# Window attention feeding a soft mixture of experts: value products over 128 keys at once, and expert weights fetched in pieces

## The chip, the cores and the metric

The kernel runs on one core of a Trainium2 chip. The metric is the device time of one execution in microseconds, the median of several runs. TensorE (PE) multiplies matrices, VectorE (DVE) and ScalarE (ACT) read its results out of PSUM, GpSimd (POOL) works on SBUF alone, and SyncE (SP) issues all the DMAs of this kernel.

## The reference

Attention over 4 batches, 8 heads, 768 positions of 64 numbers, in which a position sees the first 4 positions (sinks) and the 128 positions up to itself; its output, with the heads side by side, is the input of a soft mixture of 8 experts with 4 slots each. All is float32.

```
scores = scale * q @ k.T                       # per head, 768 x 768
keep   = (col < 4) | ((0 <= row - col) & (row - col < 128))
a      = exp(where(keep, scores, -1e9) - rowmax); a /= a.sum + 1e-9
x      = (a @ v) as 3072 x 512                  # (batch, position) x (head, dim)
logits = x @ phi                                # 3072 x 32
slot_input = softmax(logits over positions).T @ x   # 32 x 512
h      = relu(slot_input[e] @ w1[e]); slot_out = h @ w2[e]   # w1 512x1024, w2 1024x512
out    = softmax(logits over slots) @ slot_out
```

## The kernel before

**Stages.** From the start to about 211 us the kernel does the attention and the logits. The last 52 us, called the tail here, are the experts and the final product. The attention goes in 12 jobs `(b, j)`, three for each batch, of 256 positions and all 8 heads.

**One job** has these steps on PE. `prep` transposes k and q (rows `ident,first` from the buffer first_74). Four `scores` steps (S, rows `wt,qt`), each for 64 positions of both key blocks and 4 heads, go through `maxima` on DVE and `exps` on ACT. `weights_transposed` (T, rows `ident,wt`) turns the exponentials so that keys lie on partitions, and `select` on POOL makes two masked copies of them: `w = 1` for a block of 128 keys that holds the position itself, `w = 0` for the block before. `values` multiplies them by v (rows `banks<-wt 64x64`). `turned` transposes the result (rows `ident,first` from first_75), and `Moe.tokens` makes the logits (`first,phi` and `pst,vphi`), transposes them (`ident,lt`), and adds to the slots' inputs (`first,lb` and `sk,lb`). Steps of three jobs are interleaved.

**Halves of a block.** The window is 128 wide and a block of keys is 128, so for the 64 positions of half `o` one of the two blocks has all its 128 keys in play (`w = o`), and the other (`w = 1 - o`) has 64 of them; the masked remainder is zero.

**values, before.** All products have 64 keys (a quarter of the array, 64 x 64). A whole block takes two, in rows 0 to 63 and in rows 64 to 127. Two row halves must not write one PSUM bank side by side, so phase 0 pairs row half r with bank o = r and phase 1 with bank o = 1 - r. Where a phase 1 follows phase 0 of its own quad, it has a wait on some earlier DVE or ACT instruction (`guard`) or a drain of PE.

**What sets the order.** `Plan` holds a list of steps with a key (a due time, from the table `CFG`), a duration, and what each reads and writes. `Plan.order` lays them out on the engines by key and by readiness, and the program is issued in that order, with each engine's instructions in program order. All DMAs stand in the SP queue in order: a load that has to wait for a buffer holds up those behind it.

**Weights.** The 32 loads of 1 MB (w1 and w2, `Weights.load`) go to 24 buffers of 1 MB; 17 are steps of the plan, the others follow when attention's buffers come free, and the last 9 when the tail frees a buffer.

Of the kernel before, what the change touches and what calls it, by code (L numbers as in the profile page):

```python
# [19 lines left out]
P = 128  # L20
# [128 lines left out]
class Engine:  # L149


    def __init__(self, tc, engine):
        self.tc, self.engine, self.last = tc, engine, None

    def __getattr__(self, name):
        f = getattr(self.engine, name)

        def issue(*args, **kw):
            self.last = self.tc.keep_in_program_order(f(*args, **kw))  # L159
            return self.last  # L160

        return issue

# [10 lines left out]
class Plan:  # L174
# [11 lines left out]

    def __init__(self, banks):

        self.banks, self.steps, self.modes, self.aparts, self.handles, self.handed = banks, [], [], [], 0, 0

    def psum(self):
        self.handles += 1
# [15 lines left out]
    def add(self, key, eng, time, fn, r=(), w=(), new=None, last=None, mode=(128, 128), apart=None):  # L208
# [4 lines left out]
        self.aparts.append(apart)  # L213
        return len(self.steps) - 1

    def order(self):
        steps = self.steps
        writer, readers = {}, {}
        before, opener, later = [], {}, {}
        for i, (_, eng, _, _, r, w, new, last) in enumerate(steps):  # L220
            d = set()
            for x in r:
                d.add(writer.get(x, i))
                if x in opener:

                    d.update(readers.get(x, ())[-1:])
                readers.setdefault(x, []).append(i)
            for x in w:
                d.update(readers.get(x, ()))
                d.add(writer.get(x, i))  # L230
                writer[x], readers[x] = i, []
            d.discard(i)
            before.append(d)
            for x in new:
                opener[x["name"]] = i

            for x in r + w:
                if x in opener and eng != "P":
                    o = opener[x]
                    later.setdefault(o, set()).update(y for y in d if steps[y][1] == "P" and y != o and self.aparts[y] != o)  # L240
        self.before = before
# [6 lines left out]
        banks = [(0.0, i) for i in range(self.banks.shape[1])]  # L248
# [5 lines left out]
        while len(order) < len(steps):  # L254
# [27 lines left out]
            _, e, t0, i = best  # L282
            if e == "P":
                t0 += self.SWITCH * (self.modes[i] != mode)
                mode = self.modes[i][0:2]
            _, engs, times, _, _, _, new, last = steps[i]
            done.add(i)
            for x in engs:
# [13 lines left out]
            order.append((t0, len(order), i, e))  # L302
        return order

    def issue(self, engines):
        order = sorted(self.order())
        at, seen = {}, []
        end = max(t for t, _, i, e in order if e == "P" and self.steps[i][0] < self.IDLE)
        for t, _, i, e in order:
            _, _, _, fn, _, _, new, _ = self.steps[i]  # L310
            if t > end and self.steps[i][0] >= self.IDLE:
                continue
            for x in new:
                x["tile"] = self.banks[:, x["bank"]]
            if e == "P" and self.aparts[i] is not None:
                after = at[self.aparts[i]]
                self.guard = min(((z, ins) for z, p, ins in seen if p > after and z <= t), key=lambda x: x[0], default=(0, None))[1]
            fn(e)
            if e == "P":
                at[i] = len(at)  # L320
            elif e in "AV":
                p = max((at[y] for y in self.before[i] if self.steps[y][1] == "P"), default=-1)
                seen.append((t + self.steps[i][2][self.steps[i][1].index(e)], p, engines[e].last))


class InOrder(Plan):


    def add(self, key, eng, time, fn, r=(), w=(), new=None, last=None, mode=None, apart=None):
# [388 lines left out]
class Weights:  # L718
# [6 lines left out]
        self.order = first[:8] + second[:9] + first[8:] + second[9:]  # L725

    def load(self, t):
        kind, e, h = self.order[len(self.tiles)]
        if kind == 0:
            t2, w = t.rearrange("p (k m) -> p k m", k=2), self.w1[e:e + 2].rearrange("e (k p) m -> p e k m", p=P)[:, :, h, :]  # L730
        else:
            t2 = t.rearrange("p (k m) -> p k m", k=8)
            w = self.w2[e].rearrange("(p k) m -> p k m", p=P)[:, :, 256 * h:256 * h + 256]
        self.nc.sync.dma_start(t2, w)
        self.tiles.append(t)
        self.at[kind, e, h] = t


NSLOT = 24
WARM = 8, 10, 64  # L740
PT = 3
CFG = {'prep': [-2.99, 12.6],
 'load': [-5.66, -19.55],
 'v': [-1.2, -2.66],
 'S': -3.87,
 'M': -3.77,
 'E': -2.73,
 'N': [13.44, 53.07],
 'K0': -3.8,
 'T': [0.47, -19.7],  # L750
 'K': 29.21,
 'sel': [-17.71, 7.32, 4.91, 11.98],
 'val': [0.6, -4.15, 12.57, -13.52, -65.89],
 'xn': [1.21],
 'tok': [3.19, -16.24, 15.51, -3.34, 8.11, -1.71, -0.63, -5.02, 1.48, 1.1, 8.3],
 'sm': 1.41,
 'sinks': -2.62,
 'tr': [-31.47, 5.9, 6.73, -3.57, -49.94, -13.07, -0.19, 8.19, 6.09, -3.17, -12.06, 0.68, -1.67, -12.04,
        -4.42, 1.98, 59.56, -19.18, -20.81, 12.46, -40.38, -6.51, -6.05, 3.08, -20.05, 3.97, 63.44],
 'w': [33.2, 0.6],  # L760
 'fin': [8.45, 12.86, -4.85, -31.93, -19.39, -64.74, 1.63, -6.42, 62.33, 9.53, -17.38],
 'xn1': [21.29],
 'tok1': [17.06, -7.8, -20.78, 8.19, -2.53, 2.36, 1.06, -1.06, 3.59, 20.68, 1.52]}


def window_path(ctx, tc, c, moe, q, k, v, phi, w1, w2, out):
# [229 lines left out]
    def values(keys, n):  # L996
# [1 line left out]
        b, j = jobs[n]  # L998
        hs = plan.psum(), plan.psum()
        names = [h["name"] for h in hs]  # L1000
        prior = None

        def go(quad, phase):
            guard = plan.guard if phase > quad else None
            if phase > quad and guard is None:
                nc.tensor.drain()
            for a in range(4):
                y = 64 * (4 * quad + a)
                for w in (1, 0):
                    for r in range(2):  # L1010
                        o = r ^ phase
                        rows = slice(64 * r, 64 * r + 64)
                        for i in range(2):
                            if phase and w != o or (w == 0 and i == 0 and j == 0):
                                continue
                            ins = nc.tensor.matmul(
                                hs[o]["tile"][64 * i:64 * i + 64, y:y + 64],
                                lhsT=xws[quad][rows, i, w, a, 64 * o:64 * o + 64],
                                rhs=vbs[rows, (2 * n + i - 1 + w) % 4, 4 * quad + a, :],
                                start=(phase == 0 and quad == 0 and a == 0 and w == 1),  # L1020
                                stop=(phase == 1 and quad == 1 and a == 3), skip_group_check=True)
                            if guard:
                                tc.add_manual_dep(ins.ins, guard.ins.name, mybir.DependencyInfo(
                                    mybir.DependencyClass.Sync, mybir.DependencyReason.DATA), reason="row tiles")
                                guard = None

        for phase in range(2):
            for quad in range(2):
                r = [("xw", quad, i, w) for i in range(2) for w in range(2)]
                r += [("vb", x % 4) for x in range(2 * n - (j > 0), 2 * n + 2)]  # L1030
                turn = phase > quad
                prior = add(keys[2 * phase + quad], "P", 0.53 if phase else 1.0,
                            lambda e, quad=quad, phase=phase: go(quad, phase), r=r, w=names,
                            new=hs if not phase and not quad else None, mode=(*QUARTERS, 1) if turn else QUARTERS,
                            apart=prior if turn else None)
# [19 lines left out]
    def weight():  # L1055
        weights.load(slot())
# [48 lines left out]
            last = ["sit"] if b == B - 1 else []  # L1105
            moe.slot_softmax(plan, t(O["sm"]), b, [("lg", b, x, i) for x in range(NJ) for i in range(2)] + last)
    for i in range(NSLOT - 7):
        add(O["w"][0] + O["w"][1] * i, "D", 3.0, lambda e: weight())
# [14 lines left out]


def window_rest(tc, moe, plan, weight, weights, wts, slot, out):
    plan.issue({"A": moe.nc.scalar, "V": moe.nc.vector})

    def more(n):
        for _ in range(n):
# [213 lines left out]
```

## Time and profile before

| | before |
|---|---|
| median of 3 runs | 262.34 us (261.74 to 263.29) |
| the profiled execution: its time, its span | 265.25 us, 263.5 us |
| busy: PE, DVE, ACT, POOL | 216.1, 150.7, 135.4, 88.0 us |
| granted clock of TensorE, mean (1 is full speed) | 0.933 |
| DMA | 59.70 MB, 227 GB/s over the span |

The profiled execution is 2.91 us above the median, and 1.75 us of its time lie outside the span. A float32 matmul stands in the trace as two records of PE (MATMUL) and two of PEld (LDWEIGHTS); a transpose is one of each. A busy time is a sum over stages that have different limits, so the sections below go by stretches.

### The profile page before, as it was taken

How to read it: one execution, taken by the hardware profiler on the slowest of the kernel's cores; microseconds unless marked ns; L12 is line 12 of the kernel's file. 1: busy time of each engine (PE TensorE's matmuls, PEld its weight loads, DVE VectorE, ACT ScalarE, POOL GpSimd, SP SyncE). 2: the span in 40 equal slices, each digit the busy share in tenths (PEclk: the TensorE clock that was granted, in tenths of full speed). 3: DMA queues.
4: the chain of work that ended last, by engine and by line, in shares of the span. 5: the costliest groups of instructions: out<-in, count | busy, mean ns of one | idle time of the engine just before them, and what ended most of it. 6: DMA issues, size and time to landing. Idle time of an engine off the chain costs nothing.

```text
span 263.5 us, 12375 instructions
## 1 busy us (share of the span) xinstructions
PE 216.1 (82%) x5305; PEld 171.5 (65%) x5305; DVE 150.7 (57%) x368; ACT 135.4 (51%) x561; POOL 88.0 (33%) x223
## 2 busy tenths in 40 slices
PE   7679979998989778868699559958789999999820
PEld 7669857887868567757578458746669832586510
DVE  4387846888978558974459528864614331225230
ACT  2483956776767457772538437785423401224220
POOL 3133732725362443451308025351645205000000
PEclk9997999999999799995979968999979999999985
DMA  5598793889779892985729937999458769999995
GB/s 128 129 231 159 227 253 102 179 249 214 223 230 263 189 345 61 207 231 117 208 47 276 243 87 157 279 348 262 147 219 298 240 226 381 348 348 354 358 313 187
DMA packets 102979, 59.70 MB, mean 227 GB/s; under 512 B 76292, under 2 KB 98820, under 8 KB 102916
## 3 DMA queue, kind: packets, MB, share of 16 engines
q1 hardware_dynamic: 102916, 58.83, 79.4%
q8 instruction: 44, 0.72, 1.2%
q14 instruction: 19, 0.16, 0.2%
HBM read 52.53 MB, written 6.29 MB: 223 GB/s over the span
## 4 chain that ended last, share of the span: by engine, by line
PE 72%; issue 12%; DMA 5%; DVE 4%; ACT 2%; POOL 0%; DVEq 0%; ACTq 0%; POOLq 0%
PE banks L159 71%; DMA wt<-in_moe_w_dram 5%; ACT wt L159 2%; PE banks L1295 1%; DVE wt L695 1%; DVE wt L159 1%; DVE banks L159 1%; DVE first L159 1%; DVE acc L159 0%; ACT first L159 0%; DVE wt L680 0%; DVE qt L159 0%; ACT wt L679 0%; DVE si L159 0%; POOL ident masks.py:199 0%
## 5 line engine op out<-in xcount | busy, mean ns | idle before, releaser
L159 ACT ACTIVATE wt<-banks,wt 128x132 f32<-128x132 f32 x192 | 68.5, 374 | 32.3 <-DVE wt L159 22.5
L159 PE MATMUL banks<-wt 64*64 64x64 f32 (+2 forms) x2404 | 67.5, 248 | 11.6 <-issue 9.8
L159 PEld LDWEIGHTS banks<-wt 64*64 64x64 f32 (+2 forms) x2404 | 56.6, 140 | 24.1 <-issue 16.3
L159 PE MATMUL banks<-wt,qt 64*64 64x196 f32 (+2 forms) x780 | 50.4, 337 | 10.8 <-issue 7.1
L159 POOL TENSOR_SCALAR_AFFINE_SELECT wt<-wt 128x512 f32<-128x512 f32 x88 | 53.5, 634 | 14.2 <-ACT wt L159 11.6
L159 PEld LDWEIGHTS banks<-wt,qt 64*64 64x64 f32 x780 | 31.3, 140 | 15.6 <-issue 8.5
L159 ACT ACTIVATION_READ_ACCUMULATOR wt<-banks,wt 128x1 f32 x192 | 40.1, 209 | 0.0
L159 DVE TENSOR_REDUCE wt<-banks 128x4 f32<-128x528 f32 x48 | 34.0, 708 | 1.7
L159 POOL COPY sk<-wt 128x16 f32<-128x16 f32 x48 | 9.4, 197 | 72.8 <-ACT wt L159 69.5
L159 DVE COPY_PREDICATED banks<-later,banks 128x256 f32<-128x256 uint8 x48 | 20.4, 426 | 18.5 <-PE banks L159 15.2
L159 ACT COPY wt<-banks 128x512 f32<-128x512 f32 (+1 forms) x43 | 23.2, 576 | 14.5 <-PE banks L159 14.2
L159 PE MATMUL banks<-ident,first 64*128 64x64 f32 x576 | 25.5, 237 | 5.8 <-issue 4.7
L159 PEld LDWEIGHTS banks<-ident,first 64*128 64x128 f32 x576 | 22.2, 147 | 8.6 <-issue 5.3
L159 PE MATMUL banks<-ident,wt 64*128 64x64 f32 (+1 forms) x419 | 25.7, 246 | 1.2 <-issue 0.9
L159 PEld LDWEIGHTS banks<-ident,wt 64*128 64x128 f32 (+1 forms) x419 | 19.7, 150 | 8.9 <-issue 6.6
L159 DVE COPY wt<-banks 128x512 f32<-128x512 f32 (+2 forms) x34 | 21.8, 644 | 4.9 <-PE banks L159 2.6
L159 DVE TENSOR_TENSOR first<-banks,wt 128x512 f32<-128x512 f32 x24 | 15.4, 684 | 7.2 <-PE banks L159 6.8
L159 PE MATMUL banks<-first,phi 128*32 128x128 f32 x384 | 15.5, 307 | 3.9 <-issue 1.9
L159 PEld LDWEIGHTS banks<-first,phi 128*32 128x32 f32 x384 | 11.4, 122 | 5.3 <-ACT first L159 2.2
L159 PE MATMUL banks<-wt,si 128*32 128x512 f32 x112 | 14.1, 594 | 0.5 <-DVE si L159 0.5
L159 PE MATMUL banks<-neg,ident 64*64 64x68 f32 (+1 forms) x128 | 12.2, 248 | 0.2 <-issue 0.2
L159 DVE COPY first<-banks 128x512 f32<-128x512 f32 x12 | 8.2, 687 | 4.0 <-PE banks L159 3.9
(125 smaller groups left out, 228.2 us busy)
## 6 DMA issues: line engine op xcount, KB each, us to landing
wt<-in_moe_w_dram SPq DMA_DIRECT2D x30, 1024.0 KB, 9.2
wt<-in_v_dram SPq DMA_DIRECT2D x24, 256.0 KB, 4.5
first<-in_k_dram SPq DMA_DIRECT2D x22, 256.0 KB, 5.6
first<-in_q_dram SPq DMA_DIRECT2D x22, 256.0 KB, 4.6
out_dram<-wt SPq DMA_DIRECT2D x4, 1024.0 KB, 8.1
first<-in_moe_w_dram SPq DMA_DIRECT2D x2, 1024.0 KB
out_dram<-wt SPq DMA_DIRECT2D x3, 512.0 KB
first<-in_k_dram SPq DMA_DIRECT2D x4, 128.0 KB, 2.3
```

What stands on the lines that cost most here:

```text
L159: self.last = self.tc.keep_in_program_order(f(*args, **kw))
L695: (nc.vector.tensor_copy if n % 2 else nc.scalar.copy)(ob[:, 2 * (n - n0):2 * (n - n0) + 2], yp)
L1295: nc.tensor.matmul(t[:, 0:P], lhsT=c.ident, rhs=c.ident, start=True, stop=True)
```

## The change

1. `values` has four steps instead of two phases of two: for each quad `whole` multiplies the whole block with all 128 keys in one product (128 x 64 of the array) and `masked` multiplies the other with 64 keys (a quarter). The row half is o in both, so the banks need no pairing, and `guard` and the drain are gone, with the code that served them. The order is whole 0, masked 0, whole 1, masked 1.
2. A load of weights is 2 DMAs of 512 KB (w1) or 4 DMAs of 256 KB (w2), and each is a step of the plan of its own.
3. All the keys in `CFG` are other numbers, so all engines have another order. The first weights are due at 1.04 and then every 1.46, where they were due from 33.2 on, every 0.6.

```diff
-        def go(quad, phase):
-            guard = plan.guard if phase > quad else None
-            if phase > quad and guard is None:
-                nc.tensor.drain()
...
-                            if phase and w != o or (w == 0 and i == 0 and j == 0):
-                                continue
-                            ins = nc.tensor.matmul(
-                                hs[o]["tile"][64 * i:64 * i + 64, y:y + 64],
-                                lhsT=xws[quad][rows, i, w, a, 64 * o:64 * o + 64],
...
+        def product(quad, a, i, o, w, rows, start):
+            y = 64 * (4 * quad + a)
+            nc.tensor.matmul(hs[o]["tile"][64 * i:64 * i + 64, y:y + 64], lhsT=xws[quad][rows, i, w, a, 64 * o:64 * o + 64],
+                             rhs=vbs[rows, (2 * n + i - 1 + w) % 4, 4 * quad + a, :], start=start, stop=True,
+                             skip_group_check=True)
...
+                        if o or i or j:
+                            product(quad, a, i, o, o, slice(0, P), quad == 0 and a == 0)
...
+                        if not o or i or j:
+                            product(quad, a, i, o, 1 - o, slice(64 * o, 64 * o + 64),
+                                    quad == 0 and a == 0 and not (o or i or j))
...
+            add(keys[2 * quad], "P", 0.97, lambda e, quad=quad: whole(quad), r=r, w=names, new=None if quad else hs, mode=HALVES)
+            add(keys[2 * quad + 1], "P", 0.53, lambda e, quad=quad: masked(quad), r=r, w=names, mode=QUARTERS)
...
+            t, w = t[:, 1024 * x:1024 * x + 1024], self.w1[e + x, P * h:P * h + P]
...
+            t = t[:, 512 * x:512 * x + 512].rearrange("p (k m) -> p k m", k=2)
...
- 'val': [0.6, -4.15, 12.57, -13.52, -65.89],
+ 'val': [-7.87, 6.1, 1.92, -2.69, -35.19],
...
- 'w': [33.2, 0.6],
+ 'w': [1.04, 5.84],
```

How the steps of a job now stand on PE, in the middle of the program. Before, in a job with j > 0, the end of one job's values and the start of the next round (`banks<-wt 64x64` are the values; one more row of 32 of them and two S stand ahead of these):

```order
L159 MATMUL banks<-wt 64x64 x32
L159 MATMUL banks<-wt,qt 64x196 x8
L159 MATMUL banks<-wt 64x64 x32
L159 MATMUL banks<-wt,qt 64x196 x8
L159 MATMUL banks<-ident,wt 128x64 x16
L159 MATMUL banks<-ident,sk_165 64x128
L159 MATMUL banks<-ident,first_75 128x64 x16
L159 MATMUL banks<-ident,first_74 128x64 x32
L159 MATMUL banks<-first_75,phi 32x128 x16
L159 MATMUL banks<-pst,vphi 32x128 x4
```

Of the change, PE at the same place of a round; the 32 values are whole 0 and masked 0, the 16 are whole 1, and masked 1 (16 more) follows behind the `first_75,lb` and `sk,lb` rows:

```order
L159 MATMUL banks<-ident,wt 128x64 x16
L159 MATMUL banks<-ident,first_75 128x64 x16
L159 MATMUL banks<-wt,qt 64x196 x16
L159 MATMUL banks<-first_75,phi 32x128 x16
L159 MATMUL banks<-pst,vphi 32x128 x4
L159 MATMUL banks<-wt,qt 64x196 x8
L159 MATMUL banks<-ident,sk_164 64x128
L159 MATMUL banks<-wt 64x64 x32
L159 MATMUL banks<-wt,qt 64x196 x8
L159 MATMUL banks<-ident,lt 128x128
L159 MATMUL banks<-wt 64x64 x16
L159 MATMUL banks<-ident,wt 128x64 x16
```

A job has 96 value matmuls before and 64 now (72 and 48 where j = 0), three of its four S now stand together ahead of the values instead of between them, and the T of the second quad and `turned` stand ahead of them.

SP, the DMA queue, in the second half of the attention. Before:

```order
L159 DMA wt<-in_moe_w_dram 128x8x256
L159 DMA first_74<-in_q_dram 128x8x64 x2
L159 DMA first_74<-in_k_dram 128x8x64 x2
L159 DMA wt<-in_moe_w_dram 128x8x256
L159 DMA wt<-in_v_dram 128x8x64 x2
```

Of the change:

```order
L159 DMA wt<-in_v_dram 128x8x64
L159 DMA first_74<-in_q_dram 128x8x64 x2
L159 DMA first_74<-in_k_dram 128x8x64 x2
L159 DMA wt<-in_moe_w_dram 128x2x256 x7
L159 DMA wt<-in_v_dram 128x8x64
```

Where one load of 1 MB stood behind a job's q and k, seven pieces of 256 KB stand now, one behind the other. Early in the program it is one or two pieces of 512 KB for a job, from the first job on, where before the first load of weights came behind the q and k loads of three jobs.

## Rows read from the trace of the kernel before

**Rows 1.** The page: busy time by engine with instructions, and the queue of kind instruction.

```profile
PE 216.1 (82%) x5305; PEld 171.5 (65%) x5305; DVE 150.7 (57%) x368; ACT 135.4 (51%) x561; POOL 88.0 (33%) x223
q8 instruction: 44, 0.72, 1.2%
```

**Rows 2.** Chain that ended last, 19.84 to 197.2: start us, us, what.

```profile
32.77 1.87 issue
...
42.14 0.44 issue
...
62.95 0.81 issue
...
76.49 1.09 issue
...
85.97 1.81 issue
...
101.32 0.93 issue
...
111.05 0.69 issue
...
116.70 2.74 issue
...
129.71 2.60 issue
...
145.50 1.81 issue
...
150.38 3.83 issue
...
175.69 2.00 issue
...
181.74 1.17 issue
...
196.00 1.11 issue
```

**Rows 3.** Busy us (instructions) of PE, PEld, DVE, ACT, POOL; clock; DMA share; GB/s.

```profile
42.58:62.94 20.36, 19.99 (x634) 17.09 (x634) 17.26 (x39) 16.05 (x69) 10.08 (x26) 1.00 0.78 191
...
111.74:116.69 4.95, 4.80 (x126) 3.86 (x127) 4.18 (x11) 3.53 (x18) 1.64 (x5) 1.00 0.95 275
119.43:129.70 10.27, 10.27 (x253) 8.09 (x253) 6.00 (x15) 4.49 (x19) 3.04 (x7) 0.70 0.82 203
...
147.31:150.37 3.06, 2.94 (x127) 2.47 (x126) 1.51 (x4) 0.02 (x1) 0.00 (x0) 1.00 0.94 273
...
19.84:197.11 177.27, 148.48 (x4431) 123.43 (x4428) 119.84 (x278) 110.00 (x478) 72.72 (x178) 0.92 0.77 205
...
220.00:230.00 10.00, 10.00 (x124) 4.47 (x120) 1.56 (x5) 1.44 (x5) 1.04 (x3) 1.00 1.08 354
```

**Rows 4.** Timeline of PE, 39 to 44.5: start, us, instruction, count, idle before.

```profile
39.34 1.16 PE L159 MATMUL banks<-wt 64*64 64x64 f32 x64
40.32 0.85 PE L159 MATMUL banks<-wt,qt 64*64 64x196 f32 x16
41.33 0.81 PE L159 MATMUL banks<-wt 64*64 64x64 f32 x38 [0.16 <-issue]
42.58 0.62 PE L159 MATMUL banks<-wt 64*64 64x64 f32 x26 [0.44 <-issue]
...
43.79 0.72 PE L159 MATMUL banks<-ident,wt 64*128 64x64 f32 x16
44.44 0.30 PE L159 MATMUL banks<-ident,sk 128*64 128x128 f32 x1
```

**Rows 5.** Timeline of the tail: the last nine loads of weights, and who waits for them.

```profile
213.73 20.96 SPq L159 DMA_DIRECT2D wt<-in_moe_w_dram  x9
...
243.91 3.64 PE L159 MATMUL banks<-wt 128*32 128x256 f32 x58 [0.18 <-DMA wt<-in_moe_w_dram]
```

More of the change, by code (lines that the diff above doesn't have):

```diff
@@ L152, in __init__ @@
     def __init__(self, tc, engine):
-        self.tc, self.engine, self.last = tc, engine, None
+        self.tc, self.engine = tc, engine
     def __getattr__(self, name):
@@ L187, in __init__ @@
     def __init__(self, banks):
-        self.banks, self.steps, self.modes, self.aparts, self.handles, self.handed = banks, [], [], [], 0, 0
+        self.banks, self.steps, self.modes, self.handles, self.handed = banks, [], [], 0, 0
     def psum(self):
@@ L206, in find, with add @@
         return [(at[i], i) for i in range(min(both)[1], min(both)[1] + 2)] if both else []
-    def add(self, key, eng, time, fn, r=(), w=(), new=None, last=None, mode=(128, 128), apart=None):
+    def add(self, key, eng, time, fn, r=(), w=(), new=None, last=None, mode=(128, 128)):
         self.steps.append((key, eng, time if isinstance(time, tuple) else (time,) * len(eng), fn,
@@ L239, in order @@
                     o = opener[x]
-                    later.setdefault(o, set()).update(y for y in d if steps[y][1] == "P" and y != o and self.aparts[y] != o)
-        self.before = before
+                    later.setdefault(o, set()).update(y for y in d if steps[y][1] == "P" and y != o and x not in steps[y][5])
         nxt, left, ready = [[] for _ in steps], [len(d) for d in before], [0.0] * len(steps)
@@ L314, in issue, with add @@
                 x["tile"] = self.banks[:, x["bank"]]
-            if e == "P" and self.aparts[i] is not None:
-                after = at[self.aparts[i]]
-                self.guard = min(((z, ins) for z, p, ins in seen if p > after and z <= t), key=lambda x: x[0], default=(0, None))[1]
             fn(e)
[L319 to L323, printed above, removed]
 class InOrder(Plan):
-    def add(self, key, eng, time, fn, r=(), w=(), new=None, last=None, mode=None, apart=None):
+    def add(self, key, eng, time, fn, r=(), w=(), new=None, last=None, mode=None):
         if new is not None:
@@ L727, in load, with begin, piece @@
     def load(self, t):
-        kind, e, h = self.order[len(self.tiles)]
+        self.begin(t)
+        for x in range(4):
+            self.piece(t, x)
+    def begin(self, t):
+        self.at[self.order[len(self.tiles)]] = t
+        self.tiles.append(t)
+    def piece(self, t, x):
+        kind, e, h = self.order[next(i for i, y in enumerate(self.tiles) if y is t)]
         if kind == 0:
-            t2, w = t.rearrange("p (k m) -> p k m", k=2), self.w1[e:e + 2].rearrange("e (k p) m -> p e k m", p=P)[:, :, h, :]
-        else:
[L732 to L736, printed above, removed]
+            if x % 2:
+                return
+            x //= 2
+            t, w = t[:, 1024 * x:1024 * x + 1024], self.w1[e + x, P * h:P * h + P]
+        else:
+            t = t[:, 512 * x:512 * x + 512].rearrange("p (k m) -> p k m", k=2)
+            w = self.w2[e].rearrange("(p k) m -> p k m", p=P)[:, 2 * x:2 * x + 2, 256 * h:256 * h + 256]
+        self.nc.sync.dma_start(t, w)
 NSLOT = 24
@@ L1027, in values @@
[L1027 to L1035, printed above, removed]
+        def product(quad, a, i, o, w, rows, start):
[3 more added lines that the diff above has]
+                             skip_group_check=True)
@@ new lines, in whole, with masked @@
+        def whole(quad):
+            for a in range(4):
+                for o in range(2):
+                    for i in range(2):
+                        if o or i or j:
+                            product(quad, a, i, o, o, slice(0, P), quad == 0 and a == 0)
+        def masked(quad):
+            for a in range(4):
+                for o in range(2):
+                    for i in range(2):
+                        if not o or i or j:
+                            product(quad, a, i, o, 1 - o, slice(64 * o, 64 * o + 64),
+                                    quad == 0 and a == 0 and not (o or i or j))
@@ L1107, in window_path, with piece @@
     for i in range(NSLOT - 7):
-        add(O["w"][0] + O["w"][1] * i, "D", 3.0, lambda e: weight())
+        tiles = []
+        for x in range(4):
+            def piece(e, x=x, tiles=tiles):
+                if not x:
+                    tiles.append(slot())
+                    weights.begin(tiles[0])
+                weights.piece(tiles[0], x)
+            add(O["w"][0] + O["w"][1] * (i + x / 4), "D", 0.75, piece, w=[("weights", i)])
     add(100.0, "D", 3.0, lambda e: weights.load(moe.first[0]), w=[("kq", x, i, y) for x in range(2) for i in range(2) for y in range(2)])
```

69 lines of the change are left out of this document (27 added, 42 removed).

## The prediction

> **What bounds the kernel now.** I read the page first: PE has 82% of the span busy, and PE and PEld together have 10,610 records [rows 1]. A busy share that high would mean that only less work on PE helps. So I asked the chain, in order of time, what PE does when it stands still in the attention. The reader is to see fourteen pieces called "issue", in which the engine waits for nothing that the profile shows, of 0.44 to 3.83 us and 22.9 us in all [rows 2]. (Smaller ones, and waits for a named engine, are left out of that list.)
>
> What are they? The timeline shows one that cuts a value step in two: 38 records, then 0.44 us of nothing, then the other 26 of its 64 [rows 4]. No dependence can stand there. The windows between such stops give the answer by their counts: 126 and 127 records, 127 and 126, 253 and 253, 634 and 634 [rows 3]. These are 253, 253, 506 and 1,268 instructions, so one, one, two and five times about 254 (some matmul records are missing from a trace). The stops sit on a grid of 256 PE instructions. The page has a queue of kind "instruction" with 44 packets and 0.72 MB, which is 16 KB a packet, and 10,610 / 44 = 241 PE instructions for each [rows 1]. So PE's program comes by DMA in blocks of 256 instructions, and at these fourteen places the next block was late.
>
> How long does a block take to come? Two windows that ended in a long stop have just one block: 111.74 to 119.43 and 147.31 to 154.21 with their stops, which is 7.7 and 6.9 us, and in both the DMA moved 275 and 273 GB/s against 205 on average [rows 2, 3]. I read that as: the block stands in line with data. From 42.58 to 62.94 five blocks took 4.07 us each at 191 GB/s, with a stop of only 0.81 us at their end [rows 2, 3]. So a block comes in something like 4 us when the DMA is calm and in 7 us when it is not, and PE's work in a block is about as long as the former.
>
> **The stage in numbers.** From 19.84 to 197.11 there are 8,859 records, so 34.6 blocks of 5.12 us. The granted clock is 0.92 there [rows 3], and as its levels are 1.2 and 2.4 GHz, the records lose 0.08 x 177 = 14 us to the lower one. The window behind the 2.74 us stop has a clock of 0.70 where the one ahead had 1.00 [rows 2, 3]: the clock falls behind long stops. Without stops and at full clock a block holds (177.3 - 22.9 - 14) / 34.6 = 4.06 us of work.
>
> **The change, part by part.**
>
> *Fewer instructions.* 8 jobs lose 32 matmuls and 4 lose 24, in all 352. A float32 matmul is 4 records, so 1,408 instructions go, 5.5 blocks, and 29.1 are left in the stage.
>
> *The same work on PE.* Before, 32 quarter matmuls take 40.32 - 39.34 = 0.98 us [rows 4], so 15.3 ns a record with four quarters side by side, 61 ns for each place. A job has three such steps, 2.94 us. Nothing in this trace shows a 128 x 64 product of 64 columns in a row of several. If each place keeps its 61 ns, two places give 30.6 ns a record, and the 32 records of `whole` take 0.98 us; with `masked` (16 quarters, 0.49 us) twice, a job has 2.94 us again: 0. The dear end is the row with two places side by side, the transposes: 16 records in 44.44 - 43.79 = 0.65 us [rows 4], 41 ns each, so 1.30 us for `whole` and 24 x 0.32 = 7.7 us in all. I take 0, as places of the same size with the same columns are the nearer row. Below 0 I see no reason. The changes of tile shape are ten in a job in both orders, since `sk` now stands ahead of `whole` with the same shape; I price them at nothing.
>
> *The stops.* The same work over fewer instructions makes a block last 140.4 / 29.1 = 4.82 us, 0.75 us more, while the next one is fetched. Each stop gets shorter by that or vanishes: 1.12, 0, 0.06, 0.34, 1.06, 0.18, 0, 1.99, 1.85, 1.06, 3.08, 1.25, 0.42, 0.36, together 12.8 us. There are 0.84 as many blocks, so 10.7 us stay: **-12.2 us**. The bounds: nothing, if the stops are not a matter of blocks, and 5.5 x 5.12 = 28 us, if the fetch sets the whole pace of the stage, as it would where each block comes later than its work is done.
>
> The Trainium skill, in "Runtime: NRT & Kernel Launch", section "Instruction fetch mechanics", says that a sequencer's instructions come in blocks of 256, the next one fetched while the current one runs, and that the cost of crossing a block is "mostly hidden". The trace agrees on the 256 and not on the hiding: 22.9 us stand on that grid. By the page's sentence this term and the clock's would be 0, and the sum -0.1 us (262.2 us), which lies in the second rival.
>
> *The clock.* 14 us hang on falls that follow stops. With half of the stop time gone I let a third of the falls go: **-4 us** (0 to -10).
>
> *The guard.* S to value steps where phase 1 follows show 0.16 us of idle time [rows 4]; nine stops of 0.15 to 0.17 us in the chain have that place: **-1.4 us**.
>
> *The weights.* SP issues in order, and the pieces of a job stand one behind the other, seven of them with 1.75 MB, so a block of instructions meets as much data as before or more in the second half, and less in the first. From both sides: -4 us if the long stops halve in the first half, +4 us if the second half gets one more of 3.83 us. I take 0. In the tail PE waits 0.18 us for the last load, and the next 58 records are behind it [rows 5]; with pieces it needs the last one only for its last quarter: **-0.2 us**.
>
> *The order.* All other steps move. One stretch looks tight. Behind masked 1 come 64 transposes (prep, T, turned: eight banks of results), and DVE and ACT must copy these and the values' own two banks before S can have banks again. Both orders have such a knot; the new one has three S behind it where `logits` stood. DVE is busy 119.8 of 177.3 us [rows 3], 10.0 us for each of about twelve jobs, so at 13.4 us a job it still has a quarter free. What waits today behind a stop hides small dependence waits, and when stops go, some come out: **+2 us** (0 to +8).
>
> Sum: -12.2 - 4 - 1.4 - 0.2 + 2 = -15.8 us. The profiled execution would go from 265.25 to 249.5 us. The median of the runs is 2.91 us below the profiled one; I take the same difference off it: 262.34 - 15.8 = **246.5 us**.
>
> **The rivals.**
>
> 1. *Fetch sets the whole pace.* For it: the mean block takes 5.12 us, more than its 4.06 us of work. Against it: of 34 borders only fourteen have a stop over 0.4 us. It gives -28 us and some clock: 234 us or less. Chance 0.06.
> 2. *The stops stay.* Block fetches are held up by data, and the same data in less time holds them up more; the longest (3.83, 2.74, 2.60) stand where the DMA is full, and seven pieces in a row fill it longer than one load. If the stops are as long as before and only 5.5 crossings of 0.66 us (22.9 / 34.6) go, with 1.4 and 0.2: -5.2 + 2 gives 259.1 us; with one stop more, 262. Chance 0.10.
> 3. *Slower: the pieces choke the tail.* From 213.73 nine loads of 9.4 MB go at 354 GB/s [rows 3, 5] in 27 us, and PE is only 0.18 us ahead of them. Every loss of rate shows in full. If pieces of 256 KB run at a rate r, the tail grows by 27 x (354 / r - 1) us; the other 15.8 us are gone at r = 223 GB/s, and below 217 GB/s it is slower than before by more than 0.5%: at 200 GB/s, 267 us. Against it: a 1 KB run for each partition and row is the same in both, and the loads stand in line, so their fixed costs overlap. Chance 0.07. The Trainium skill, "DMA: Bandwidth & Descriptors", section "Rules for kernel authors", asks for 1 MiB or more in a DMA for full bandwidth, which speaks for this rival; no run here shows pieces of 256 KB of weights.
>
> The forecast itself, with its bounds (7.7 us dearer products, +8 us for the order, half of the stops' gain on the one side; more of the clock on the other), has 0.77.
>
> **How the numbers follow.** A measurement of this kernel can tell about 0.5% (1.3 us) from no change. The range is **237 to 256 us**: the forecast with its bounds; outside it are the first rival, most of the second and the third (0.06 + 0.08 + 0.06 = 0.20). Faster by over 0.5%: 0.77 + 0.06 + half of rival 2 (0.05) = **0.88**. Within 0.5%: the other half, **0.05**. Slower: **0.07**.
>
> **What would show it.** In the profile after: about 9,200 records of PE and PEld together and some 38 or 39 packets of kind instruction; the stops still on the grid of 256, but fewer, and none over 2.5 us outside of full DMA; `whole` at 32 records in about 0.98 us; a granted clock above 0.92 in the stage; the tail about 52 us as before, at 350 GB/s. The prediction is wrong if the stops stand elsewhere, if `whole` takes more than 1.3 us, if PE waits in the tail for weights, or if named waits for DVE and ACT ahead of S grow by more than 1.3 us a job, which over twelve jobs would eat the whole gain.

## The result, and the profile after

The changed kernel took 232.25 to 241.5 us in four runs, a median of 236.03 us, and the kernel before 261.74 to 265.53 us beside it, a median of 262.81 us. The ratio is 0.883, 95% interval [0.871, 0.895]; it leaves out the two runs of 239.5 and 241.5 us, in which the clock was lower. The profiled run took 232.55 us. The gain is 27 to 31 us, where I had forecast 15.8 us and a time between 237 and 256 us: the direction was right, the size was not. Six later runs of the same kernel (below) took 232.8 to 245.5 us, so single runs lie on both sides of 237 us.

The page after, as in [rows 1]:

```profile
PE 203.7 (88%) x4607; PEld 162.7 (70%) x4607; DVE 142.7 (62%) x351; ACT 140.5 (61%) x578; POOL 85.9 (37%) x223
q8 instruction: 38, 0.62, 1.2%
```

9,214 records and 38 packets of code are what the count of products had given. One reading of the prediction needs a correction: its blocks of 254 lack no records. Counted with PE's semaphore waits and drains, which the page leaves out, the fourteen stops of [rows 2] lie whole multiples of 256 instructions apart, to within one. Next, what PE waits for from 19.84 us to the first products of the tail (us in total, times, longest); of before, 19.84 to 211.78:

```profile
PE banks L159 <- issue: 24.6, 24, 3.8
PE banks L159 <- ACT wt L159: 1.4, 1, 1.4
PE banks L159 <- DVE first L159: 1.2, 1, 1.2
PE banks L159 <- ACT first L159: 0.8, 1, 0.8
```

and of after, 19.84 to 179.54:

```profile
PE banks L159 <- issue: 2.3, 4, 1.4
PE banks L159 <- DVE qt L159: 2.2, 5, 0.6
PE banks L159 <- DVE wt L159: 1.7, 4, 0.5
PE banks L159 <- ACT wt L159: 0.7, 1, 0.7
PE banks L159 <- POOL wt L159: 0.7, 1, 0.7
```

The stops called "issue" are nearly gone, and short waits for named engines, mostly ahead of S, have taken a little of their place. The windows of the same stretch, first of before, then of after (columns as in [rows 3]):

```profile
19.84:211.78 191.94, 162.48 (x4626) 136.12 (x4623) 125.58 (x297) 114.82 (x494) 78.54 (x193) 0.93 0.77 210
```

```profile
19.84:179.54 159.70, 150.45 (x3861) 126.90 (x3861) 117.48 (x278) 119.12 (x508) 75.34 (x190) 1.00 0.93 250
```

The stage is 32.2 us shorter. The stops give 22.3 of it: before, 17 of the 24 stood at borders of blocks, 23.4 us, and seven of 0.15 to 0.16 us stood ahead of value steps, off the grid; after, four are left, all at borders. The clock gives 12.7: it stood at 1.2 GHz six times in the stage before, for 27.3 us, in which PE was busy for 25.3 us and lost half of that, and not once in this trace after. Three of the six and the sum, of before:

```profile
152.95:159.78 6.83, 5.57 (x88) 4.94 (x92) 2.88 (x5) 3.36 (x13) 1.93 (x4) 0.50 0.13 25
190.50:193.91 3.41, 3.41 (x111) 3.03 (x106) 0.78 (x3) 1.00 (x4) 1.69 (x4) 0.50 0.97 394
19.84:23.24 3.40, 3.40 (x75) 3.40 (x75) 2.01 (x7) 0.66 (x2) 2.29 (x6) 0.50 0.58 95
sum 27.28, PE 25.30 PEld 21.77 DVE 10.96 ACT 8.79 POOL 7.43; mean PE 4.22 PEld 3.63 DVE 1.83 ACT 1.46 POOL 1.24
```

Four of the six falls came within or just behind a stop at a border. The one at 190.50 stands behind a wait of 1.16 us for DVE, and the first, at 19.83, has no stop of 1 us in the 6 us ahead of it; these two are 3.4 of the 12.7 us. PE's busy time less what the low clock cost it, 162.5 - 12.7 = 149.8 us, has become 150.4 us, and the named waits of over 0.1 us went from 4.2 to 6.5 us. So -22.3 - 12.7 + 0.6 + 2.3 = -32.1 us. The tail, the other stretch in which much could happen, kept its length, of before and of after:

```profile
211.78:263.50 51.72, 38.70 (x454) 22.13 (x454) 13.92 (x32) 10.52 (x26) 3.84 (x7) 0.92 0.94 314
```

```profile
185.00:205.00 20.00, 19.88 (x249) 11.42 (x242) 4.25 (x13) 3.52 (x12) 3.80 (x7) 1.00 1.08 359
...
179.54:230.80 51.26, 38.08 (x454) 22.01 (x454) 13.92 (x32) 10.51 (x26) 3.85 (x7) 0.93 0.94 314
```

The pieces run at 359 GB/s there. One long stop is left, still inside a row of S steps (timeline of PE after):

```profile
149.43 0.57 PE L159 MATMUL banks<-wt,qt 64*64 64x196 f32 x7
151.45 0.71 PE L159 MATMUL banks<-wt,qt 64*64 64x196 f32 x9 [1.44 <-issue]
```

### The profile page after: what moved, and what is told of

It reads as the page before. It is cut to its first block, busy times and chain, and to the rows that moved or that the text cites. A ratio compares the mean times of both kernels' runs of the same rounds, so it can differ in the third digit from the quotient of the medians.

```text
span 230.8 us, 11001 instructions
## 1 busy us (share of the span) xinstructions
PE 203.7 (88%) x4607; PEld 162.7 (70%) x4607; DVE 142.7 (62%) x351; ACT 140.5 (61%) x578; POOL 85.9 (37%) x223
## 4 chain that ended last, share of the span: by engine, by line
PE 72%; DVE 12%; ACT 5%; issue 4%; POOL 3%; DVEq 0%; ACTq 0%; POOLq 0%
PE banks L159 70%; DVE wt L159 4%; ACT wt L159 4%; DVE first L159 3%; POOL wt L159 2%; PE banks L1292 2%; DVE qt L159 1%; DVE wt L682 1%; DVE acc L159 1%; ACT qt L159 1%; POOL sk L159 1%; DVE wt L667 0%; DVE banks L159 0%; ACT wt L666 0%; DVE rs L159 0%
## 5 line engine op out<-in xcount | busy, mean ns | idle before, releaser
L159 PE MATMUL banks<-wt 64*64 64x64 f32 (+2 forms) x1700 | 65.8, 251 | 2.2 <-DVE wt L667 1.0
L159 PEld LDWEIGHTS banks<-wt 64*64 64x64 f32 (+2 forms) x1700 | 52.9, 133 | 15.0 <-issue 4.6
L159 PE MATMUL banks<-wt,qt 64*64 64x196 f32 (+2 forms) x780 | 42.6, 319 | 7.7 <-DVE qt L159 2.2
L159 ACT ACTIVATION_READ_ACCUMULATOR wt<-banks,wt 128x1 f32 x192 | 41.7, 217 | 0.0
L159 ACT COPY wt<-banks 128x512 f32<-128x512 f32 (+1 forms) x55 | 30.1, 582 | 13.1 <-PE banks L159 11.6
L159 PE MATMUL banks<-ident,first 64*128 64x64 f32 x576 | 23.9, 226 | 0.4 <-DVE first L159 0.4
L159 PEld LDWEIGHTS banks<-ident,first 64*128 64x128 f32 x576 | 20.7, 138 | 2.0 <-DVE first L159 0.8
L159 DVE COPY wt<-banks 128x512 f32<-128x512 f32 (+2 forms) x22 | 13.4, 617 | 6.6 <-PE banks L159 3.5
L159 PE MATMUL banks<-first,phi 128*32 128x128 f32 x384 | 13.4, 276 | 0.5 <-issue 0.3
L159 POOL COPY wt<-wt 128x512 f32<-128x512 f32 (+3 forms) x14 | 6.1, 439 | 14.8 <-PE banks L159 7.7
L159 PE MATMUL banks<-neg,ident 64*64 64x68 f32 (+1 forms) x128 | 11.6, 245 | 0.0
```

The lines of the kernel that those rows point to most:

```text
L159: return self.tc.keep_in_program_order(f(*args, **kw))
```

## The experiments

Theories. *Instructions*: fewer PE instructions make a block of 256 last longer, so the next one is there in time. *Pieces*: code stands behind 1 MB loads, and pieces let it through. *Order*: the new table of numbers spreads the work better. The clock is held to follow from the stops in all of them.

**How a stop was measured.** Each packet of code in the trace (queue 8) was set against the 256-instruction border behind which it was sent. From a border to its packet I call the delay; the packet takes 1.1 us; and where PE had to wait, it went on 1.39 to 1.54 us after the packet's end, in the means of the runs. A stop is then delay + 1.1 + 1.4 us less the work in the block. Summed over the stage, nought where it is negative, this gives 29.8 us for before (29.8 measured from record to record), 3.5 for after (3.3), 6.5 for K=128 alone (6.9). The table has, for all blocks between about 23 us and the tail: median work of a block, mean delay, delays over 3 us; and the stops "issue" of the waits, half of the time at 1.2 GHz (13.6 here where PE lost 12.7), and the median of all runs. The stops hold some 1 us off the grid in the rows with the old quarters, and 2.8 us in that of the changed kernel with quarters.

| kernel | work | delay | over 3 us | stops | clock | median us |
|---|---|---|---|---|---|---|
| before | 4.05 | 2.17 | 6 | 24.6 | 13.6 | 261.5 to 263.7 |
| pieces alone | 3.98 | 1.93 | 4 | 22.4 | 4.4 | 254.1 |
| K=128 alone | 4.69 | 1.94 | 1 | 4.5 | 0 | 242.1 |
| both, old order | 4.76 | 1.86 | 4 | 5.4 | 1.4 | 237.7 |
| changed | 4.78 | 1.61 | 1 | 2.3 | 0 | 236.0, 237.7 |
| changed, whole loads | 4.64 | 1.92 | 5 | 5.8 | 1.7 | 242.3 |
| changed, quarters | 4.32 | 2.15 | 7 | 23.4 | 13.7 | 270.9 |
| before, half a block on | 4.06 | 2.13 | 6 | 25.0 | 8.5 | |
| K=128 alone, half a block on | 4.82 | 1.97 | 7 | 9.8 | 9.5 | |
| changed, half a block on | 4.77 | 2.11 | 6 | 10.0 | 0 | |

One trace is not the kernel: the changed program was profiled three times (in its first runs, in its later ones, and as the run of idle instructions below, which is the same program) and has stops of 2.3, 2.1 and 4.8 us, with 1, 1 and 2 delays over 3 us. Differences of 2 to 3 us of stops between two rows say nothing.

**K=128 alone.** The order and the 1 MB loads of before stand.

```diff
-    for w in (1, 0): for r in range(2): ...      # quarters, two phases
+    w = o if phase else 1 - o
+    rows = slice(0, P) if phase else slice(64 * o, 64 * o + 64)
```

> The kernel before with its order and its 1 MB loads, and K=128 in place of the quarters: the step that was the first half of a quad does its masked products (K=64), the step that was the second half does the whole ones (K=128), without guard or drain. 38 instruction packets. The theory of instructions: stops of 22.9 us fall to 12 or less, 243 to 250 us (my forecast for the whole change was 246.5 on this ground). The theory of pieces: stops stay over 15 us, 256 to 262 us. The theory of the order: 256 to 262 us, since the order stands.

Measured: 242.1 us (234.1 to 246.4), 20.5 us less than the 262.6 us beside it. PE's waits, first line, and the window:

```profile
PE banks L159 <- issue: 4.5, 7, 1.0
```

```profile
19.84:181.32 161.48, 152.05 (x3928) 128.15 (x3923) 125.72 (x297) 114.80 (x494) 78.81 (x193) 1.00 0.91 250
```

In the profiled run this one part takes away four fifths of the stops and all falls of the clock. That run is the fastest of the four, 234.1 us with a granted clock of 0.984 in the mean; the others have 0.951 to 0.970, so the clock fell in them. It speaks for the theory of instructions, and the gain is even a little over that theory's range.

**Pieces alone.** Quarters and order of before; each load is four pieces, one behind the other.

```diff
-        self.nc.sync.dma_start(t2, w)
+        for x in range(4):
+            self.piece(t, x)
```

> The kernel before with its order and its quarters; each load of weights issued as pieces of 256 or 512 KB, one behind the other, where the 1 MB load stood. The theory of pieces: the fetches no longer stand behind 1 MB, stops fall to 12 us or less, 244 to 252 us. The theories of instructions and of the order: 258 to 265 us, stops over 18 us (the same bytes at the same time).

Measured: 254.1 us, ratio 0.977 [0.959, 0.995]. The first line of the waits, and the window:

```profile
PE banks L159 <- issue: 22.4, 22, 3.9
```

```profile
19.84:201.85 182.01, 154.95 (x4623) 129.96 (x4619) 124.64 (x296) 114.30 (x493) 78.09 (x190) 0.98 0.83 221
```

The stops hardly changed, by 2.2 us; of the 9.9 us by which the stage got shorter in the profiled run, 8.4 are the clock's, which stood low for 8.8 us in place of 27.3. The time lies between the ranges of the theories, 6 us below the kernel before by the ratio and 8.5 by the medians. The stops speak against the theory of pieces, which wanted 12 us or less.

**Both, in the old order** (the two edits above together).

> The kernel before with its order, with K=128 as in the run of K=128 alone and the loads issued as pieces as in the run of pieces alone, so that only the new table is missing from the whole change. If the two parts add and the order is worth nothing: 262.6 less 20.5 less 8.5 us, 230 to 238 us, with stops under 4 us, delays from a border to the packet of code of 1.6 to 1.8 us in the mean (2.17 before, 1.94 with K=128 alone) and no fall of the clock in the attention. The theory that the new order carries part of it: 240 us or more. The theory that K=128 alone does all (pieces worth nothing once the blocks are longer): 239 to 244 us, as K=128 alone.

Measured: 237.7 us (235.0 to 238.7), ratio 0.916 [0.907, 0.924]; the changed kernel beside it (below) has the same median, and its fastest run is 2.2 us faster. So the new table is worth 2 to 3 us at most, and the theory of the order falls. The time is as expected; the stops (5.4 us) and the mean delay (1.86) are above what adding the parts had wanted, and the one fall, at 19.24, stands ahead of the first stop at a border. By the medians the two parts taken alone, 20.5 + 8.5 us, add up to 5 us more than both together gave. That would leave some 4 us to the pieces beside K=128, but the fastest runs, 234.1 us without pieces and 235.0 with them, don't show it.

**Whole loads in the changed kernel**, with every step in its place.

```diff
     def piece(self, t, x):
+        if x:
+            return          # the first piece loads the whole tile, 1 MB
```

> The changed kernel with the program order of every engine kept, and each tile of weights fetched by one 1 MB load where its first piece stood, the other pieces left out. The theory of pieces: the fetches stand behind 1 MB loads again, stops of 8 us or more up to the tail, 240 us or more. The theory of instructions: stops stay under 4 us, 231 to 236 us. The theory of the order (what cost 267 us with whole loads before was the order that the planner made anew): as that of instructions, 231 to 236 us.

Measured: 242.3 us, ratio 0.937 [0.925, 0.950]. The same program beside it with pieces (the run of idle instructions, below) took 238.3 us, so pieces are worth 4 us by the medians; the intervals of the ratios overlap (0.925 to 0.950 and 0.904 to 0.937). Stops of 5.8 us lie between what the two theories wanted (8 or more, under 4), and in the trace beside it the program with pieces has 4.8. With whole loads five delays are over 3 us, with pieces two, and the longer blocks swallow most of that.

**Quarters in the changed kernel**, with every step in its place.

```diff
-    (whole(quad), masked(quad))
+    (quarters(quad, 0), quarters(quad, 1))      # a drain ahead of all but the first
```

> The changed kernel with every step in its place, and the products of each quad in quarters again: the first step does 32 products of K=64, the second 16, with a drain ahead of each but the first of a job. 44 instruction packets. The theory of instructions (work on a block of 256 against the fetch): the median work of a block falls from 4.8 to about 4.1 us, stops of 15 to 25 us together, falls of the clock behind those over 2.5 us, 250 to 260 us. The theory of pieces: stops under 10 us, 238 to 246 us. The drains themselves: 3 a job at no more than 0.3 us, 0 to 11 us in all, seen in the stops ahead of the product steps off the grid.

Measured: 270.9 us (259.5 to 279.1), above both ranges. Of its profile the first line of the waits, a stop that cuts a product step, and the windows ahead of it and behind it:

```profile
PE banks L159 <- issue: 23.4, 31, 3.4
```

```profile
82.66 0.81 PE L159 MATMUL banks<-wt 64*64 64x64 f32 x40
86.69 0.58 PE L159 MATMUL banks<-wt 64*64 64x64 f32 x24 [3.21 <-issue]
...
89.40 1.13 PE L159 MATMUL banks<-wt 64*64 64x64 f32 x32 [0.24 <-issue]
```

```profile
79.00:83.40 4.40, 4.06 (x157) 3.12 (x154) 2.48 (x7) 4.20 (x24) 0.00 (x0) 1.00 1.02 305
87.60:91.00 3.40, 3.16 (x68) 2.37 (x66) 1.74 (x4) 2.10 (x9) 1.75 (x6) 0.51 0.03 7
```

The reader sees the whole mechanism in these lines: DMA at 305 GB/s ahead, a stop of 3.21 us in the middle of 64 products, and half the clock 0.95 us after its end, with the DMA idle by then. Of the 23.4 us, 20.6 stand at borders; the rest are 13 stops of 0.16 to 0.24 us off the grid, ahead of value steps, of which 36 have a drain. With the order and the pieces held fast, the count of instructions carries the change from one side of the limit to the other.

**Weights out of the way, before.** The 17 loads of the attention are issued behind the last job's loads; nothing else moves.

```diff
-        add(O["w"][0] + O["w"][1] * i, "D", 3.0, lambda e: weight())
+        add(O["w"][0] + O["w"][1] * i, "D", 3.0, lambda e: held.append(1))
```

> The kernel before with its 17 loads of weights of the attention issued only behind the last job's loads, so that no load of weights stands beside the first jobs; nothing else moves in the program. The tail then waits for the weights, and its time and that of the whole say nothing on the change; the stage from 19.84 us to the first products of the tail is read. The theory that instructions alone set the stops: they stay at 15 to 23 us up to there. The theory that code fetches stand behind the loads of weights: stops under 8 us, no packet later than 3 us behind its border in the jobs without such loads, and the clock over 0.97 there.

Measured: 281 us, most of it a tail that waits. Read up to the last job's `logits`: from the first transposes to there it took 165.93 - 6.88 = 159.05 us, and 189.86 - 7.73 = 182.13 us before, on the same PE program. PE's waits up to 168 us:

```profile
PE banks L159 <- issue: 9.4, 21, 1.2
```

No delay there was over 3 us, and after 21.5 us the clock did not fall. So this stretch gets 23 us shorter without a change to one product, 14 us of them stops (23.4 us before): the delays are made by data. The 9.4 us left are more than the theory's 8 us, but on its side.

**Three parts left out one at a time, planned anew.** Here the table's numbers were kept, and the planner made its order again from steps that they were not made for.

> The changed kernel with the weights fetched in whole loads of 1 MB again; the K=128 products and the new table stay. The theory of instructions (the stops at the 256 grid went because each product step has half the instructions, so there is more work for each block of 256): 230 to 238 us, stops together under 5 us. The theory of pieces (the 1 MB loads are what the code fetches stood behind, 3.4 to 5.2 us from border to packet before): the stops come back in good part, 10 us or more, and 243 to 255 us. The theory of the order (the new table spreads loads and steps): as the first, 230 to 238.

> The changed kernel with the table of numbers of the kernel before (the four product keys assigned by half: whole 0.6 and -4.15, masked 12.57 and -13.52); K=128 products and pieces stay. The theory of instructions and that of pieces: 228 to 242 us, stops under 5 us, clock 0.97 or more. The theory of the order: 248 to 258 us, most of the 30 us of the change lost.

> The changed kernel with the products in K=64 quarters again, with drains and guards as in the kernel before; pieces and the new table stay (its four product keys assigned by half). 44 instruction packets again. The theory of instructions: stops of 12 to 22 us, the half clock behind them, 252 to 262 us. The theory of pieces: stops under 8 us, 236 to 246 us (the guards' 1.4 us and the second half of the rows' cost back). The theory of the order: 236 to 244 us.

Measured: 267.2, 271.2 and 284.0 us, all slower than before, and outside of every theory. PE's waits of the second:

```profile
PE banks L159 <- ACT wt L159: 5.7, 11, 1.1
PE banks L159 <- POOL wt L159: 4.1, 9, 1.7
PE banks L159 <- ACT first L159: 3.9, 6, 1.7
```

22 us of named waits and only 2.5 us of stops: in this one the order was bad, not the part left out. (The first has stops of 15.5 us and the third 19.4 us beside theirs.) A table of keys belongs to its steps, and taken alone these three would have told that every part carries the whole gain. They are why the other runs keep the order.

**Idle instructions.** Sixty-four instructions without work behind each K=128 step were to bring the count back.

```diff
+            for _ in range(64 if j else 56):
+                nc.tensor.nop(nofuse=True)
```

> The changed kernel with the program order of the PE kept and 64 instructions without work (56 in the first job of a batch row) behind each of the two K=128 product steps of a job, so that the count of instructions is again that of the kernel before (44 instruction packets for 38). The theory of instructions: stops of 10 to 20 us come back at the 256 grid, and 245 to 260 us. The theory of pieces and that of the order: no stops beyond 4 us together; the idle instructions themselves cost at most 64 times some 15 ns, 1 us a step, of which the waits ahead of S take a part, 232 to 248 us. The stops at the grid tell the two apart more than the time does.

The page has 38 packets, and the borders stand at the same records as in the changed kernel: the idle instructions are not in the program that ran. So it tells nothing of instructions and is the changed kernel again, 236.7 to 238.5 us in three runs (a fourth, of 464.9 us, is an outlier). Whether instructions without work would have brought the stops back stays open.

**All pieces of 256 KB, and the changed kernel again.**

```diff
-            x //= 2
-            t, w = t[:, 1024 * x:1024 * x + 1024], self.w1[e + x, P * h:P * h + P]
+            z = 512 * (x % 2)
+            t, w = t[:, 512 * x:512 * x + 512], self.w1[e + x // 2, P * h:P * h + P, z:z + 512]
```

> The changed kernel with the 512 KB pieces halved too, so that all weights come in pieces of 256 KB. The theory that a fetch of code waits for what lies ahead of it in the queues: the mean delay falls below 1.6 us, the last long stop (1.44 us behind a delay of 3.41) goes, 1 to 3 us faster than the changed kernel, and the tail stays at 51 to 52 us. The theory that the size of a piece has done all it can: no difference beyond 1 us. If the issue of more pieces on SP binds (28 more in some 230 us): slower by 1 to 4 us, in the tail.

> The changed kernel itself once more, beside the others on the same chip: 231 to 241 us, as in its first runs; where it is at the upper end, stops over 2 us and a fall of the clock in the attention, where at the lower end neither.

Measured: 236.1 us (234.0 to 237.0), and 237.7 us (232.8 to 245.5). No delay over 3 us with the smaller pieces, but stops and mean delay (1.69 and 1.65 us) are the same. The medians cannot be told apart; what differs is the spread, 3.0 us against 12.7 in six runs each. The two runs of the changed kernel at 245 us have a granted clock of 0.949 and 0.955 in the mean, where its fastest have 0.983 to 0.985: so the falls come back in some of its executions.

**The borders moved.** 32 (in one run 16) products of two columns ahead of the program.

```diff
+    for _ in range(32):
+        nc.tensor.matmul(t[:, 0:2], lhsT=c.ident, rhs=c.ident[:, 0:2], start=True, stop=True)
```

> The kernel before with 32 products of two columns ahead of the program, which move every border of 256 PE instructions by half a block; nothing else. The theory of places (a delay is long where a border happens to fall into a burst of data): the number of delays over 3 us is another one, 1 to 9 for 6, the stops 15 to 30 us, the time 250 to 268 us, and the long stops stand elsewhere. The theory of length (short blocks make long delays, wherever they begin): 5 to 7 delays over 3 us, stops of 22 to 28 us, 260 to 267 us.

> The kernel before with 16 products of two columns ahead of the program: the borders move by a quarter of a block. Theories and numbers as for the shift by half a block; the theory of places also expects that the two shifts differ from one another by 4 us or more of stops, that of length that they agree within 3 us.

> The run of K=128 alone (old order, 1 MB loads) with its borders moved by half a block. The theory of places: delays over 3 us come back (3 to 8 for 1), stops of 8 to 15 us for 4.5, 243 to 254 us. The theory of length: at most 2 such delays, stops of 3 to 7 us, 238 to 244 us.

> The changed kernel with its borders moved by half a block. The theory of places: 0 to 5 delays over 3 us, but with 4.8 us of work in a block and pieces the stops stay at 2 to 8 us, 233 to 244 us. The theory of length: as the changed kernel, stops of 2 to 4 us, 232 to 238 us.

Measured: 279.6, 269.3, 256.2 and 255.3 us. All lie above what both theories had, since the shift was not free: the first transposes come 8 to 15 us later. About half of that is the clock. In the shifted K=128 kernel the products of two columns took 0.11 us a record at full clock, and 0.21 behind a fall in the middle of them:

```profile
4.64:8.05 3.41, 3.41 (x34) 3.41 (x32) 0.96 (x7) 0.00 (x0) 0.00 (x0) 1.00 0.92 208
8.05:18.60 10.55, 10.55 (x51) 10.55 (x51) 0.00 (x0) 0.00 (x0) 0.00 (x0) 0.50 0.22 47
```

The other three have 0.21 us from the start and no record of the granted clock until 1.3 to 1.7 us behind their first transposes. The timeline of PE in the shifted changed kernel (in the unshifted one the 18 transposes take 2.29 us):

```profile
5.11 13.65 PE L1294 MATMUL banks<-ident 128*128 128x2 f32 x64
18.62 4.19 PE L159 MATMUL banks<-ident 128*128 128x128 f32 x18
22.74 1.12 PE L159 MATMUL banks<-ident,first 64*128 64x64 f32 x16
```

So the stretch from the first transposes to the first products of the tail is compared: before 204.0 us, shifted by a half 202.4, by a quarter 198.8; K=128 alone 173.4, shifted 187.2; changed 172.2, shifted 179.9. The last one's window and first line of waits:

```profile
22.74:202.63 179.89, 161.98 (x4120) 136.19 (x4119) 126.29 (x297) 128.84 (x550) 80.03 (x202) 1.00 0.87 232
```

```profile
PE banks L159 <- issue: 10.0, 11, 2.0
```

Long delays are back in both kernels with K=128 (1 to 7, 1 to 6), as the theory of places wanted. The kernel before has about its usual number in all three places, and stops of 24.6, 25.0 and 23.2 us, as the theory of length wanted; but short blocks are not needed for long delays, so that theory falls for the kernels with K=128. The unshifted changed program has 172.2, 172.7 and 176.7 us in its three traces, so 3 to 8 of its 32 us are the luck (or the choice) of where its borders fall. What stays in the other place is 202.4 - 179.9 = 22.5 us. As the start took longer, the loads also stand 8 to 15 us earlier against PE's work, so what moved is the place of the borders against the loads, and no run moved the borders alone.

## Why the prediction was wrong in size

*What bounds the kernel*, the grid of 256 and the late code: right. The weights out of the way show that the delays are data, the quarters in the new order that the work in a block of instructions decides whether a delay becomes a stop.

*The stops* (-12.2 us) is the step that failed first: -22.3 us measured, 21.2 of them at borders. Its reasoning priced one of two things. Take 0.64 us, the growth of the median work of a block with K=128 alone, off each stop of before, and 29.8 us become 18.2: -11.6 us, about my number. But I kept each delay as long as it was. In the changed kernel the mean delay is 1.61 us for 2.17, and over 3 us there is one for six. With pieces it is a little shorter (1.94 to 1.86 and 1.92 to 1.61 with K=128, 2.17 to 1.93 without), and the places of the borders count (2.11 with the borders moved, where the stops fall from 25.0 to 10.0 us, 15 us, nearer to my term). So the part beyond 12 us is in part luck of these places. I had the bound for this, 28 us, and took it to need a fetch that sets the whole pace.

*The clock* (-4 us): -12.7 us measured. I let a third of the falls go, with half of the stop time. By the traces, what counts is how many stops are long. In the 18 traces, from 19.84 us to the tail, there are 19 stops of over 2.3 us, and 16 of them have a fall within them or within 1.3 us after; of 87 of 1 to 2.3 us 14 do. The first trace of the changed kernel has none of over 2.3 us, and no fall. My own shortened list had one such stop left, and by it most of the falls should have gone. That stops make falls is read from these places, for 30 of 41 falls; the other 11 have no such stop ahead of them, and their cause is open. No run changed the clock alone.

*The weights in pieces* (0, -4 to +4): 0 to -4 us beside K=128, where the medians show a gain and the fastest runs none; -6 to -8.5 us beside quarters, most of it the clock's. In this change the term holds within its bounds.

*The same work* (0): +0.6 us in the stage, but not as priced. At full clock the value products went from 38.5 to 41.9 us and the other rows gave back 2.8, 1.1 of it a row that now stands ahead of 19.84 us. `whole` takes 1.08 us (50.16 to 51.24 in the timeline), up to 1.30 where it stands behind `sk`, for 0.98, and `masked` 0.52 to 0.63 for 0.49.

*The order* (+2): +2.3 us of named waits, as priced; the old order with the same parts has no such growth (4.2 us) and the same median. *The tail*: -0.5 us for -0.2. *The guard* (-1.4): seven stops off the grid, 1.1 us, are gone.

Rival 1 came near the number (its 234 us or less holds for two of the four runs), but not the mechanism: only 4 of some 30 blocks stop in the changed kernel, so the fetch does not set the pace. Rival 2 falls with the stops. Rival 3 falls with 359 GB/s in the tail: what the Trainium skill, "DMA: Bandwidth & Descriptors", section "Rules for kernel authors", asks for, 1 MiB in a DMA, was not needed by pieces that stand in line. And the Trainium skill's "mostly hidden", in "Runtime: NRT & Kernel Launch", section "Instruction fetch mechanics", is true of the changed kernel's first trace (2.3 us of stops) and not with its borders moved (10.0 us at the same 4.8 us of work in a block). The prediction's sum by that sentence has a slip: its other terms, -1.4 - 0.2 + 2, give +0.4 us and 262.7 us, not -0.1 and 262.2.

## What to carry to other kernels

Where PE stands still for "issue" at multiples of 256 PE instructions (records, semaphore waits and drains together), compare the work in such a block with the time that its successor needs (here 1.6 to 2.2 us of delay, 1.1 of packet, 1.4 to go on): a few tenths of a microsecond of work more in a block can be worth more than the work itself, since the clock falls behind the long stops too. Price both sides, the block's work and the data that stands ahead of the code, and expect several us from the mere place of the borders against the loads. When a planner makes the order, test a part with the order held fast, or the new order is what is measured.

## What the runs showed of the hardware that was not expected

A product of two columns of 128 rows in a row of such took as long as one of 128 columns: 13.65 us for 64 records, 0.21 us each, against 4.19 / 18 = 0.23 us in the same place, and 0.11 us at full clock against 2.29 / 18 = 0.13. Of 36 value steps with a drain ahead of them, 13 had a stop of 0.16 to 0.24 us. Code waits behind data even at 1.1 us of its own: 17 loads moved away took the longest delay from 5.23 to 2.55 us.
